# Transposing all of x by DMA rather than the first four tiles on TensorE, in a gated mix of linear attention and a token MLP

## The chip, the cores and the metric

The kernel runs on one core of a Trainium2 chip. The metric is the device time of one execution in microseconds (us), as a median. Traces have their own zero, the start of the span; a span is about 2 us shorter than the run's time. One first execution of the kernel before (963.45 us) is left out everywhere.

## The reference, cut to what matters

```
x: 2048 x 512, bf16 (16 tiles of 128 rows)
qkv = x @ wqkv;  phi(t) = where(t > 0, t + 1, exp(t)) + 1e-6
kv  = sum over s of phi(k)^T v        # per head, 32 heads of 16
a   = (phi(q) kv / phi(q) z) @ wo
b   = token MLP over the sequence of layernorm(x)   # 2048 -> 1792 -> 2048, gelu
g   = sigmoid(sum(x * gate_w));  out = g * a + (1 - g) * b
```

Only the first stage matters here: K = x Wk with its feature map phi, and G = x^T phi(K), tile by tile, with the layer-norm statistics of x beside them. K needs x transposed (`xT`), G and the statistics need plain x (`xs`).

Of the kernel before, what the change touches and what calls it, by code (L numbers as in the profile page):

```python
# [7 lines left out]
ACT = mybir.ActivationFunctionType  # L8
ALU = mybir.AluOpType
AX = mybir.AxisListType  # L10
BF16 = mybir.dt.bfloat16
# [4 lines left out]
def kernel(  # L16
# [13 lines left out]
    nc = tc.nc  # L30
    P = nc.NUM_PARTITIONS
# [8 lines left out]
    NT = S // P  # L40
    ND = D // P
# [22 lines left out]
    def keep(shape, dtype, name):  # L64
        return persist.tile(shape, dtype, name=name, tag=name)

    def bank(name, dtype=FP32):
        return ps.tile([P, SC], dtype, name=name, tag="bank")

    xs = keep([P, NT, D], BF16, "xs")  # L70
    hs = keep([P, NT, D], BF16, "hs")
    xT = keep([P, ND, S], BF16, "xT")
    wq_sb = keep([P, ND, D], BF16, "wq_sb")
    wk_sb = keep([P, ND, D], BF16, "wk_sb")
# [3 lines left out]
    pk = keep([P, NT, D], BF16, "pk")  # L78
# [9 lines left out]
    ident = keep([P, P], BF16, "ident")  # L88
# [18 lines left out]
    def mm(o, lhsT, rhs, start, stop, **kw):  # L107
        nc.tensor.matmul(o, lhsT=lhsT, rhs=rhs, start=start, stop=stop, **kw)  # L108
# [14 lines left out]
    def load_x(q, t0, n):  # L123
        q.dma_start(out=xs[:, t0 : t0 + n, :], in_=x_view[:, t0 : t0 + n, :])

    def load_wk(q, k):
        q.dma_start(out=wk_sb[:, k, :], in_=wqkv_view[:, k, D : 2 * D])

    def load_xT(t0, n):
        nc.sync.dma_start(  # L130
            out=xT[:, :, t0 * P : (t0 + n) * P], in_=X[t0 * P : (t0 + n) * P, :], transpose=True
        )

    load_x(nc.sync, 0, 1)
    load_x(nc.scalar, 1, 1)
    load_wk(nc.sync, 0)
    load_x(nc.scalar, 2, 1)
    load_x(nc.sync, 3, 1)
    for k, q in ((1, nc.scalar), (2, nc.sync), (3, nc.scalar)):
        load_wk(q, k)  # L140
    load_xT(4, 2)
    load_xT(6, 2)
    load_x(nc.sync, 4, 4)
# [5 lines left out]
    for c, (j0, nb) in enumerate(w1_chunks):  # L149
        w = wpool.tile([P, NT, FB * P], BF16, name="w1c", tag="wc")  # L150
        w1c.append(w)
        for t0 in range(0, NT, 8) if c == 0 else (0,):
            t1 = t0 + 8 if c == 0 else NT
            nc.sync.dma_start(
                out=w[:, t0:t1, : nb * P], in_=w1_view[:, t0:t1, j0 * P : (j0 + nb) * P]
# [11 lines left out]
        out=ident[:], in_=ident[:], compare_op=ALU.not_equal, fill=1.0, base=0,  # L167
# [7 lines left out]
    def load_small():  # L175
        nc.gpsimd.dma_start(out=brow[0:NF, :], in_=B_b1.rearrange("(f q) -> f q", q=P))
        nc.gpsimd.dma_start(out=brow[NF : NF + NT, :], in_=B_b2.rearrange("(f q) -> f q", q=P))
        nc.gpsimd.dma_start(
            out=gw_b[:], in_=gate_w.rearrange("(o d) -> o d", o=1).to_broadcast([P, D])
        )  # L180
# [3 lines left out]
    def warm_up(n, cols=SC):  # L184
        for _ in range(n):
            mm(wps[:, :cols], warm[:, 0:P], warm[:, :cols], True, True)

    act_warm = keep([P, 1], FP32, "act_warm")
    nc.scalar.activation(out=act_warm[:], in_=ones_f[:], func=ACT.Exp)
    warm_up(6)  # L190

    def transpose_tile(t, on_act):
        pt = bank("pt", BF16)
        for k in range(ND):
            nc.tensor.transpose(pt[:, k * P : (k + 1) * P], xs[:, t, k * P : (k + 1) * P], ident[:])  # L195
        dst = xT[:, :, t * P : (t + 1) * P]
        src = pt[:].rearrange("p (k s) -> p k s", k=ND)
        if on_act:
            nc.scalar.activation(out=dst, in_=src, func=ACT.Copy)  # L199
        else:  # L200
            nc.vector.tensor_copy(out=dst, in_=src)

    def phi(dst, acc):
        e = work.tile([P, SC], BF16, name="e", tag="e", bufs=6)
        nc.scalar.activation(out=e[:], in_=acc[:], func=ACT.Exp)  # L205
        nc.vector.tensor_scalar(  # L206
            out=e[:], in0=e[:], scalar1=1.0, scalar2=PHI_EPS, op0=ALU.min, op1=ALU.add
        )
        nc.vector.scalar_tensor_tensor(  # L209
            out=dst, in0=acc[:], scalar=0.0, in1=e[:], op0=ALU.max, op1=ALU.add  # L210
        )

    kaccs = {}

    def k_part(t, ks):
        if t not in kaccs:
            kaccs[t] = bank("kacc")
        for k in ks:
            mm(
                kaccs[t][:], xT[:, k, t * P : (t + 1) * P], wk_sb[:, k, :],  # L220
                k == 0, k == ND - 1,
            )

    def k_phi(t):
        phi(pk[:, t, :], kaccs.pop(t))

    def ln_stats(t):
        stats = work.tile([P, nc.vector.BN_STATS_DIM], FP32, name="stats", tag="stats", bufs=2)
        nc.vector.bn_stats(out=stats[:], in_=xs[:, t, :])  # L229
        nc.vector.bn_aggr(out=mv[:, t, :], in_=stats[:])  # L230

    def ln_rstd(g):
        s = slice(g * TPC, (g + 1) * TPC)
        nc.vector.tensor_scalar_add(out=veps[:, s], in0=mv[:, s, 1], scalar1=EPS)
        nc.gpsimd.tensor_tensor(out=rstd[:, s], in0=veps[:, s], in1=mhalf[:], op=ALU.pow)

    def ln_shift(g):
        s = slice(g * TPC, (g + 1) * TPC)
        nc.vector.scalar_tensor_tensor(  # L239
            out=nmr[:, s], in0=mv[:, s, 0], scalar=-1.0, in1=rstd[:, s],  # L240
            op0=ALU.mult, op1=ALU.mult,
        )

    def ln_apply(t):
        nc.scalar.activation(  # L245
            out=hs[:, t, :], in_=xs[:, t, :], func=ACT.Identity,
            scale=rstd[:, t : t + 1], bias=nmr[:, t : t + 1],
        )
# [3 lines left out]
    def g_tile(t):  # L252
        if not gacc:
            gacc.extend(bank("gacc") for _ in range(ND))
        for k in range(ND):
            mm(gacc[k][:], xs[:, t, k * P : (k + 1) * P], pk[:, t, :], t == 0, t == NT - 1)
# [15 lines left out]
    def ln_step(u):  # L272
        ln_stats(u)
        if u % TPC == TPC - 1:
            ln_rstd(u // TPC)

    HEADS = 4
    transpose_tile(0, False)
    transpose_tile(1, True)
    transpose_tile(2, False)  # L280
    ln_step(0)
    for k in range(2):
        for t in range(HEADS - 1):
            k_part(t, (k,))
    transpose_tile(HEADS - 1, True)
    ln_step(1)
    for t in range(HEADS):
        k_part(t, range(2 if t < HEADS - 1 else 0, ND))
        k_phi(t)
    LAG = 4  # L290
    LN_LAG = 3
    APPLY = 9
    for t in range(HEADS, NT):
        k_part(t, range(ND))
        k_phi(t)
        g_tile(t - LAG)
        if t > LAG:
            ln_step(t - LN_LAG)
        if t == TPC - 1 + LN_LAG:
            load_small()  # L300
        if t >= APPLY:
            ln_apply(t - APPLY)
        if t % TPC == 0 and t >= 2 * TPC:
            ln_shift(t // TPC - 2)
# [129 lines left out]
    for j in range(NB0, NF):  # L434
# [20 lines left out]
        out=gg[:], in0=gth[:], scalar1=0.5, scalar2=0.5, op0=ALU.mult, op1=ALU.add  # L455
    )
    nc.vector.tensor_scalar(
        out=c1[:], in0=gth[:], scalar1=-0.5, scalar2=0.5, op0=ALU.mult, op1=ALU.add
# [3 lines left out]
    for t in range(NT):  # L462
        c, tl = divmod(t, TPC)
        aps = bank("aps")
        for j in range(ND):
# [3 lines left out]
            out=a_sc[:], in_=aps[:], func=ACT.Identity,  # L469
            scale=gg[:, t : t + 1], bias=c2[:, t : t + 1],  # L470
        )
        for c0, W in ((0, D - P), (D - P, P)) if t == NT - 1 else ((0, D),):
            cs = slice(c0, c0 + W)
            yps = bank("yps")
            for f in range(NF):
# [6 lines left out]
                out=ot[:, :W], in0=yps[:, :W], scalar=c1[:, t : t + 1], in1=a_sc[:, cs],  # L482
# [35 lines left out]
```

## The kernel before: the parts that the change touches

The loads at the start. SP and ACT issue on two DMA rings. Tiles 0 to 3 are loaded plain, and the four chunks of Wk between them; the other tiles are transposed by the DMA.

```python
load_x(nc.sync, 0, 1)
load_x(nc.scalar, 1, 1)
load_wk(nc.sync, 0)
load_x(nc.scalar, 2, 1)
load_x(nc.sync, 3, 1)
for k, q in ((1, nc.scalar), (2, nc.sync), (3, nc.scalar)):
    load_wk(q, k)
load_xT(4, 2)          # DMA transpose of tiles 4, 5
load_xT(6, 2)
load_x(nc.sync, 4, 4)
...                    # tiles 8 to 15 in fours, then Wq, w1, Wv, Wo
```

TensorE transposes tiles 0 to 3 through PSUM, and the first chunks of Wk are used for three tiles while the others are still under way:

```python
HEADS = 4
transpose_tile(0, False); transpose_tile(1, True); transpose_tile(2, False)
ln_step(0)                                # statistics of tile 0
for k in range(2):
    for t in range(HEADS - 1):
        k_part(t, (k,))
transpose_tile(HEADS - 1, True)
ln_step(1)
for t in range(HEADS):
    k_part(t, range(2 if t < HEADS - 1 else 0, ND))
    k_phi(t)                              # exp on ACT, two steps on VectorE -> pk
LAG, LN_LAG = 4, 3
for t in range(HEADS, NT):
    k_part(t, range(ND)); k_phi(t)
    g_tile(t - LAG)                       # G needs pk of tile t - 4
    if t > LAG: ln_step(t - LN_LAG)
    ...
```

(`transpose_tile` is four PE transposes of 128x128 into a PSUM bank and one copy into `xT`, on ACT or VectorE.)

## Time and profile before

| | before |
|---|---|
| median | 165.75 us (165.62 to 165.82) |
| TensorE busy | 97% of the span |
| first stage (K and G) ends | 33.19 us |
| from there to the end of the span | 130.21 us |

The next fence is a table of stretches for the kernel before: the stretch, its length, busy us and number of instructions for TensorE, its weight loads, VectorE, ACT and GpSimd, then the granted clock, the mean share of the DMA engines and GB/s. A share over 1 is packets that overlap.

```profile
3.00:4.00 1.00, 0.72 (x4) 0.17 (x3) 0.00 (x0) 0.99 (x2) 0.17 (x2) 1.00 1.04 346
4.00:5.00 1.00, 1.00 (x12) 1.00 (x11) 0.42 (x1) 0.26 (x2) 0.00 (x0) 1.00 1.05 336
...
7.00:8.00 1.00, 1.00 (x8) 0.41 (x6) 0.33 (x2) 0.89 (x2) 0.00 (x0) 1.00 1.23 192
...
33.19:163.40 130.21, 126.77 (x641) 58.59 (x650) 61.75 (x132) 40.93 (x62) 11.13 (x18) 1.00 0.41 125
```

Plain loads alone move 346 GB/s; the microsecond in which almost only transposes run (7 to 8 us) moves 192 GB/s at a full share. The last line is all that comes after the first stage.

### The profile page before, as it was taken

To read this page: it belongs to the slowest core of one execution; us is meant where nothing else is said; L and a number is where in the kernel's file an instruction comes from. 1 tells how busy PE (TensorE), PEld (TensorE's weight loads), DVE (VectorE), ACT (ScalarE), POOL (GpSimd) and SP (SyncE) were. 2 spreads that over 40 slices of the span, in tenths; PEclk is the share of its full clock that TensorE was granted. 3 is DMA by queue.
4 is the path that set the end of the run, shared out by engine and by line. 5 is a ranking of instruction groups with operands and counts; after the bars stand their busy time and mean duration, and the time that the engine had idled before them with its cause. 6 is when DMAs were issued, how large, how long until landed. Compare 5 with 4: busy or idle time off the path is not lost.

```text
span 163.4 us, 2099 instructions
## 1 busy us (share of the span) xinstructions
PE 158.7 (97%) x787; PEld 73.3 (45%) x801; DVE 88.3 (54%) x202; ACT 58.7 (36%) x90; POOL 18.3 (11%) x37
## 2 busy tenths in 40 slices
PE   7999999999999999999999999999999999999993
PEld 2544444444444444444444444444444444444452
DVE  1599999957999999029995301156221111111112
ACT  3463386648676483111222213111112222111110
POOL 5000711200100000001055500050000000000000
PEclk9999999999999999999999999999999999999999
DMA  5999999999950007600893599932100000111001
GB/s 152 235 237 213 280 308 328 349 349 348 326 130 0 0 0 247 202 4 0 286 299 101 181 320 279 323 121 88 36 32 32 32 32 32 45 52 35 32 32 32
DMA packets 30057, 25.05 MB, mean 153 GB/s; under 512 B 7968, under 2 KB 29472, under 8 KB 30048
## 3 DMA queue, kind: packets, MB, share of 16 engines
q1 hardware_dynamic: 28032, 22.02, 45.5%
q0 software_dynamic: 1440, 2.38, 5.5%
q10 hardware_dynamic: 576, 0.52, 1.1%
q8 instruction: 6, 0.10, 0.3%
q14 instruction: 3, 0.02, 0.0%
HBM read 21.11 MB, written 2.23 MB: 143 GB/s over the span
## 4 chain that ended last, share of the span: by engine, by line
PE 95%; DMA 2%; issue 1%; ACT 0%; DVE 0%
PE uacc L108 30%; PE yps L108 29%; PE aps L108 9%; PE gacc L108 8%; PE qacc L108 8%; PE kacc L108 8%; DMA xs<-in_A_x_dram 2%; PE pt L195 1%; PE denps L108 1%; PE wps L108 1%; PE kvps L108 0%; ACT xT L199 0%; DVE ot L481 0%; PE zps L108 0%; PE pt L324 0%
## 5 line engine op out<-in xcount | busy, mean ns | idle before, releaser
L108 PE MATMUL uacc<-hs,w1c 128*128 128x512 bf16 x219 | 51.8, 379 | 0.4
L108 PE MATMUL yps<-uT,w2c 128*128 128x512 bf16 (+2 forms) x234 | 50.6, 366 | 0.2
L481 DVE SCALAR_TENSOR_TENSOR ot<-yps,c,a_sc 128x512 bf16<-128x512 f32 (+2 forms) x17 | 12.2, 720 | 46.0 <-PE yps L108 42.7
L108 PEld LDWEIGHTS <-w2c 128*128 128x128 bf16 x238 | 22.8, 98 | 25.9
L108 PEld LDWEIGHTS <-w1c 128*128 128x128 bf16 x224 | 21.7, 98 | 26.3 <-issue 0.4
L468 ACT ACTIVATE a_sc<-aps,c,gg 128x512 f32<-128x512 f32 x16 | 12.4, 778 | 46.7 <-PE aps L108 43.0
L318 ACT ACTIVATE uT<-uacc,bcol 128x512 bf16<-128x512 f32 x14 | 9.3, 687 | 28.3 <-PE uacc L108 28.3
L108 PE MATMUL aps<-W2sb,pqT 128*128 128x512 bf16 x63 | 16.4, 379 | 0.1
L108 PE MATMUL qacc<-xT,wq_sb 128*128 128x512 bf16 x63 | 16.2, 379 | 0.0
L108 PE MATMUL kacc<-wk_sb,xT 128*128 128x512 bf16 x63 | 16.0, 380 | 0.1
L108 PE MATMUL gacc<-pk,xs 128*128 128x512 bf16 x62 | 15.5, 379 | 0.1
L245 ACT ACTIVATE hs<-xs,nmr,rstd 128x512 bf16<-128x512 bf16 x16 | 12.8, 805 | 1.9 <-DVE nmr L239 1.9
L205 ACT ACTIVATE e<-qacc 128x512 bf16<-128x512 f32 x16 | 9.6, 597 | 9.2 <-PE qacc L108 8.3
L419 POOL DMA_DIRECT2D rex<-rd_dram x16 | 9.4, 602 | 23.0 <-DVE pqT L421 17.5
L205 ACT ACTIVATE e<-kacc 128x512 bf16<-128x512 f32 x16 | 9.3, 595 | 6.9 <-PE kacc L108 5.6
L209 DVE SCALAR_TENSOR_TENSOR pk<-kacc,e 128x512 bf16<-128x512 f32 x16 | 11.1, 692 | 0.6
L209 DVE SCALAR_TENSOR_TENSOR pqT<-qacc,e 128x512 bf16<-128x512 f32 x16 | 11.1, 692 | 0.6
L229 DVE BATCH_NORM_STATS2 stats<-xs 128x6 f32<-128x512 bf16 x16 | 10.9, 682 | 0.0
L206 DVE TENSOR_SCALAR e<-e 128x512 bf16<-128x512 bf16 x32 | 9.0, 282 | 3.1 <-ACT e L205 3.1
L406 DVE CUSTOM_DVE_ANT_0 junk<-xs,gw_b 128x512 bf16<-128x512 bf16 x16 | 9.9, 684 | 0.0
L270 DVE TENSOR_TENSOR zacc<-zacc,pk 128x512 f32<-128x512 f32 x14 | 9.6, 686 | 0.2
L108 PEld LDWEIGHTS <-pqT 128*128 128x128 bf16 x64 | 6.3, 98 | 7.6
(65 smaller groups left out, 69.6 us busy)
## 6 DMA issues: line engine op xcount, KB each, us to landing
w2c<-in_B_w_dram SPq DMA_DIRECT2D x8, 896.0 KB, 6.6
w1c<-in_B_w_dram SPq DMA_DIRECT2D x2, 2048.0 KB, 15.7
w1c<-in_B_w_dram SPq DMA_DIRECT2D x3, 1024.0 KB, 12.9
rex<-rd_dram POOLq DMA_DIRECT2D x16, 128.0 KB, 3.2
out_dram<-ot SPq DMA_DIRECT2D x15, 128.0 KB, 1.7
xs<-in_A_x_dram SPq DMA_DIRECT2D x3, 512.0 KB, 5.1
wq_sb<-in_A_wqkv_dram SPq DMA_DIRECT2D x1, 512.0 KB, 7.1
wv_sb<-in_A_wqkv_dram SPq DMA_DIRECT2D x1, 512.0 KB, 11.4
```

The costliest lines, as they stand in the source:

```text
L108: nc.tensor.matmul(o, lhsT=lhsT, rhs=rhs, start=start, stop=stop, **kw)
L205: nc.scalar.activation(out=e[:], in_=acc[:], func=ACT.Exp)
L206: nc.vector.tensor_scalar(out=e[:], in0=e[:], scalar1=1.0, scalar2=PHI_EPS, op0=ALU.min, op1=ALU.add)
L209: nc.vector.scalar_tensor_tensor(out=dst, in0=acc[:], scalar=0.0, in1=e[:], op0=ALU.max, op1=ALU.add)
L229: nc.vector.bn_stats(out=stats[:], in_=xs[:, t, :])
L245: nc.scalar.activation(out=hs[:, t, :], in_=xs[:, t, :], func=ACT.Identity, scale=rstd[:, t : t + 1], bias=nmr[:, t : t + 1],)
L270: nc.vector.tensor_tensor(out=zacc[:], in0=first, in1=pk[:, t, :], op=ALU.add)
L318: nc.scalar.activation(out=uT[:, j, :], in_=acc[:], func=ACT.Gelu_apprx_tanh, bias=bcol[:, j : j + 1])
L406: nc.vector.tensor_tensor_reduce(out=junk[:], in0=xs[:, t, :], in1=gw_b[:], scale=1.0, scalar=0.0, op0=ALU.mult, op1=ALU.add, accum_out=gp ...
L419: nc.gpsimd.dma_start(out=rex[:], in_=src.unsqueeze(1).to_broadcast([8, HEAD, SC]))
L468: nc.scalar.activation(out=a_sc[:], in_=aps[:], func=ACT.Identity, scale=gg[:, t : t + 1], bias=c2[:, t : t + 1],)
L481: nc.vector.scalar_tensor_tensor(out=ot[:, :W], in0=yps[:, :W], scalar=c1[:, t : t + 1], in1=a_sc[:, cs], op0=ALU.mult, op1=ALU.add,)
```

## The change

Its intent is to take the 16 transposes and their copies off the start of TensorE's work: the DMA transposes x anyhow for the later tiles, so let it do so for all. Tiles 0 and 1 come by a transpose each, ahead of everything on SP; Wk and the plain tiles 0 to 3 go to ACT's ring.

```diff
-    load_x(nc.sync, 0, 1)
-    load_x(nc.scalar, 1, 1)
-    load_wk(nc.sync, 0)
-    load_x(nc.scalar, 2, 1)
-    load_x(nc.sync, 3, 1)
-    for k, q in ((1, nc.scalar), (2, nc.sync), (3, nc.scalar)):
-        load_wk(q, k)
+    load_xT(0, 1)
+    load_wk(nc.scalar, 0)
+    load_xT(1, 1)
+    for k in range(1, ND):
+        load_wk(nc.scalar, k)
+    load_xT(2, 2)
+    load_x(nc.scalar, 0, 4)
     load_xT(4, 2)
...
-    warm_up(6)
+    warm_up(7)
...                      (transpose_tile and the interleaved head of the loop are removed)
-    for t in range(HEADS, NT):
-        k_part(t, range(ND))
-        k_phi(t)
-        g_tile(t - LAG)
-        if t > LAG:
+    for t in range(NT):
+        k_block(t)
+        if t >= LAG:
+            g_tile(t - LAG)
+        if t >= LN_LAG:
             ln_step(t - LN_LAG)
```

More of the change, by code (lines that the diff above doesn't have):

```diff
@@ L189 @@
     nc.scalar.activation(out=act_warm[:], in_=ones_f[:], func=ACT.Exp)
-    warm_up(6)
-    def transpose_tile(t, on_act):
-        pt = bank("pt", BF16)
-        for k in range(ND):
-            nc.tensor.transpose(pt[:, k * P : (k + 1) * P], xs[:, t, k * P : (k + 1) * P], ident[:])
-        dst = xT[:, :, t * P : (t + 1) * P]
-        src = pt[:].rearrange("p (k s) -> p k s", k=ND)
-        if on_act:
-            nc.scalar.activation(out=dst, in_=src, func=ACT.Copy)
-        else:
-            nc.vector.tensor_copy(out=dst, in_=src)
+    warm_up(7)
     def phi(dst, acc):
@@ L211, in phi, with k_block @@
         )
-    kaccs = {}
-    def k_part(t, ks):
-        if t not in kaccs:
-            kaccs[t] = bank("kacc")
-        for k in ks:
-            mm(
-                kaccs[t][:], xT[:, k, t * P : (t + 1) * P], wk_sb[:, k, :],
-                k == 0, k == ND - 1,
-            )
-    def k_phi(t):
-        phi(pk[:, t, :], kaccs.pop(t))
+    def k_block(t):
+        kacc = bank("kacc")
+        for k in range(ND):
+            mm(kacc[:], xT[:, k, t * P : (t + 1) * P], wk_sb[:, k, :], k == 0, k == ND - 1)
+        phi(pk[:, t, :], kacc)
     def ln_stats(t):
@@ L275, in ln_step @@
             ln_rstd(u // TPC)
-    HEADS = 4
-    transpose_tile(0, False)
-    transpose_tile(1, True)
-    transpose_tile(2, False)
-    ln_step(0)
-    for k in range(2):
-        for t in range(HEADS - 1):
-            k_part(t, (k,))
-    transpose_tile(HEADS - 1, True)
-    ln_step(1)
-    for t in range(HEADS):
-        k_part(t, range(2 if t < HEADS - 1 else 0, ND))
-        k_phi(t)
     LAG = 4
@@ L292 @@
     APPLY = 9
-    for t in range(HEADS, NT):
-        k_part(t, range(ND))
-        k_phi(t)
-        g_tile(t - LAG)
-        if t > LAG:
+    for t in range(NT):
[3 more added lines that the diff above has]
+        if t >= LN_LAG:
             ln_step(t - LN_LAG)
```

## The prediction

> **What bounds the kernel now.** I began with the page's busy shares and chain of waits. They settle where a gain can lie at all: TensorE is busy for 97% of the span, and the chain that ended last is 95% TensorE work.
>
> ```profile
> PE 158.7 (97%) x787; PEld 73.3 (45%) x801; DVE 88.3 (54%) x202; ACT 58.7 (36%) x90; POOL 18.3 (11%) x37
> PE 95%; DMA 2%; issue 1%; ACT 0%; DVE 0%
> ```
>
> What is not TensorE work on that chain is the first load. So I read the same chain in order of time (start, length, what) for the first 11 us, which is all that the change touches.
>
> ```profile
> 0.81 2.98 DMA xs<-in_A_x_dram
> 3.79 0.05 issue
> 3.84 1.05 PE pt L195 x8
> 4.89 0.02 issue
> 4.91 0.61 ACT xT L199
> 5.51 0.05 issue
> 5.56 1.29 PE kacc L108 x5
> 6.85 0.22 PE pt L195 x4
> 7.08 3.02 PE kacc L108 x14
> ```
>
> See here that nothing can start before 3.84 us, when the first tile of x has landed, and that transposing and copying out cost the chain 1.05 + 0.61 + 0.22 = 1.9 us up to 7.08. From there on it is only the K and G matmuls, four in 0.86 us (0.216 us each), until 33.19 us. The stage from the first landing to its end takes 33.19 - 3.84 = 29.35 us; its 128 K and G matmuls need 128 x 0.216 = 27.6 us. So the whole overhead of the beginning, as the kernel stands, is 1.7 us, 1% of 165.8 us.
>
> The third view is VectorE's timeline in this stage, because the page's slices show it at 9 tenths there (start, length, operation; the last lines are the end of the stage).
>
> ```profile
> 8.23 0.29 DVE L206 TENSOR_SCALAR e<-e 128x512 bf16<-128x512 bf16 x1 [0.86 <-ACT e L205]
> 8.56 0.69 DVE L209 SCALAR_TENSOR_TENSOR pk<-kacc,e 128x512 bf16<-128x512 f32 x1
> 9.17 0.28 DVE L206 TENSOR_SCALAR e<-e 128x512 bf16<-128x512 bf16 x1
> ...
> 20.07 0.29 DVE L206 TENSOR_SCALAR e<-e 128x512 bf16<-128x512 bf16 x1
> 20.39 0.69 DVE L209 SCALAR_TENSOR_TENSOR pk<-kacc,e 128x512 bf16<-128x512 f32 x1
> 21.00 0.69 DVE L229 BATCH_NORM_STATS2 stats<-xs 128x6 f32<-128x512 bf16 x1
> 21.71 0.18 DVE L230 BATCH_NORM_AGGREGATE mv<-stats 128x2 f32<-128x6 f32 x1
> 21.81 0.26 DVE L206 TENSOR_SCALAR e<-e 128x512 bf16<-128x512 bf16 x1
> ...
> 31.22 0.69 DVE L209 SCALAR_TENSOR_TENSOR pk<-kacc,e 128x512 bf16<-128x512 f32 x1
> ```
>
> A feature-map pair alone repeats every 0.93 us (8.23 to 9.17); with one layer-norm statistic it repeats every 1.74 us (20.07 to 21.81). TensorE's period is 8 x 0.216 = 1.73 us for a K and a G tile. The two engines are level, and VectorE idles nowhere from 8.23 us on. The last pk ends at 31.91 us; the G matmuls that read it start at 33.19 - 0.86 = 32.33 us. VectorE's slack at the end of the stage is thus 0.42 us. I think this is the number that decides the case.
>
> **What the Trainium skill says.** "DMA: Bandwidth & Descriptors", section "Issuing engines are not separate DMA queues", says that transfers started from different engines run on the same 16 DMA engines and interleave, and only issue time is saved. The trace agrees: from 3 to 5 us, with both rings in use, the DMA share is full at 346 and 336 GB/s. Moving the Wk chunks to ACT's ring therefore makes no bandwidth.
>
> The same page, section "Latency and other measured facts", gives DMA transposes an effective 261 GB/s. In the trace the two transposes of 256 rows (256 KB each) were issued at 3.62 and 4.97 us and landed 4.1 and 3.7 us later, at 7.7 and 8.7 us: 256 KB in 1.0 us, about 260 GB/s. It agrees, and is less than the plain loads' 346.
>
> "TensorE: Matmul & The Clock Gate", Part 1, says that matmuls run at half rate until the array has been busy for a window of about 3.4 us, and that the window runs freely. The trace has the warm-up matmuls 0.43 us apart, the first K matmul at 5.09 us at 420 ns and those after 5.5 us at 379 ns, so full rate came about 4.5 us after the first warm-up matmul. The profile's PEclk row doesn't show this. Part 4 of that page says that PE transposes do not count as busy in the same way; no run so far shows it either way.
>
> **The change part by part.**
>
> Removed from TensorE: 16 transposes. Twelve took 3.84 to 5.09 us, 1.25 us, and four took 0.22 us: 1.47 us, plus the waits for their copies. Removed beside it: two copies on ACT (2 x 0.60 us) and two on VectorE (2 x 0.42 us). VectorE's were in idle time.
>
> Added: three transposes by DMA (128, 128, 256 rows) on SP, in place of four plain loads; the plain tiles 0 to 3 are loaded too, in one piece of 512 KB, for G and the layer norm. So 0.5 MB more is moved in all, early, where the DMA engines are full. One more warm-up matmul (0.43 us) ends at about 0.84 + 7 x 0.43 = 3.9 us, before data comes: free.
>
> When does TensorE start? An issue of 256 rows took SP 1.3 us and landed 2.4 to 2.8 us after its end. For 128 rows I take half the issue, 0.65 us, and the same tail: 0.81 + 0.65 + 2.4 to 2.8 = 3.9 to 4.3 us. The Wk chunks leave ACT at about 0.80, 1.25, 1.70 and 2.15 us; before, chunks took 3.1 to 4.3 us to land, in order of issue. With that I get about 3.9, 4.6, 5.3 and 6.0 us. Here the order of work matters: before, three tiles used chunks 0 and 1 while 2 and 3 were under way; now tile 0 goes through all four chunks first. So K of tile 0 is done when chunk 3 has landed and one matmul has run: about 6.2 us. The 31 K and G groups after it need 124 x 0.216 = 26.8 us, so TensorE alone would end the stage at 33.0 us, 0.2 us earlier than now. The 1.5 us of transposes mostly turn into a wait for Wk.
>
> When does VectorE start and end? ACT's queue now issues the 512 KB load only when chunk 0 has landed (its semaphore is reused; the order of instructions shows it). That is about 4.0 + 0.6 us; then the table load, 1.28 us, and the small activation, 0.2 us: ACT is free at about 6.1 us and doesn't hold up the first exponential. That runs at 6.6 to 7.2 us (0.4 us for the last matmul's own latency, 0.60 us for itself), so VectorE begins at about 7.2 us, a microsecond earlier than 8.23. But the statistics of tiles 0 and 1, which fell in idle time before, now come into the saturated stretch: 2 x (1.74 - 0.93) = 1.6 us. Before, the stretch took 31.91 - 8.23 = 23.7 us; it becomes 25.3 us, and the last pk ends at 32.5 us. The last G tile ends 0.86 us and some 0.1 us of signal later: 33.5 us, 0.3 us **later** than now. That is above TensorE's 33.0 us and hence sets the end.
>
> Everything after this stage is unchanged TensorE work and moves with it. The sum is 165.8 + 0.3 = 166.1 us. I add 0.2 us for the risk below that is one-sided and say 166.3 us.
>
> **The rivals.**
>
> *The clock stays at half rate longer.* The warm-up now ends at 3.9 us and TensorE is then starved until about 6 us. If the window that gave full rate at about 5.3 us is not busy enough, full rate comes one window later, at about 8.7 us. Between 6.2 and 8.7 us TensorE would do 6 matmuls rather than 12, which costs 1.2 us: 167 to 167.5 us. For it: a starved array; against it: the matmuls that do run in the gap. I give it one in three.
>
> *The plain tiles 0 to 3 become the wait.* The first G group and the statistics need them at about 6.2 + 4 x 0.86 = 9.6 us. Issued at about 4.2 us, with the 4.8 to 5.1 us that such loads took, they land at 9.0 to 9.3 us. Transposes share the engines, so 1 to 2 us of stall are possible: 167 to 168 us.
>
> *A real gain.* If Wk lands faster, as ACT's ring is now Wk's alone, and K of tile 0 ends at 5.3 us, TensorE alone would end at 32.1 us, 1.1 us earlier. But VectorE would have to begin by 8.23 + 0.42 - 1.6 = 7.0 us just to break even, and ACT isn't free before about 6.1 us, so 6.7 us is the earliest: at most 0.3 us better, 165.5 us.
>
> *First transposes slow.* If a DMA transpose at the very beginning needs 5 us or more, everything slips by the excess. Nothing in the trace shows it; over 2% would take 3.3 us.
>
> **Range and chances.** The gain is capped at about 0.3 to 0.5 us by VectorE, the losses reach 2 us: 165.3 to 168.0 us. Over 2% faster (below 162.5 us) exceeds the whole overhead of 1.7 us: 0.01. Over 2% slower (above 169.1 us) needs two of the rivals together: 0.05. Within 2%: 0.94.
>
> **What would show it.** The first K matmul at about 4 us and tile 0's fourth at about 6 us, waiting for Wk; the first feature map on VectorE at about 7.2 us and then no idle time to the end; the last G tile waiting for pk; the stage's end at about 33.5 us. Matmul starts 0.43 us apart after 6 us would mean the clock rival; G's first weight load waiting on x's DMA, the second. I am wrong if the stage ends more than 2 us from 33.5 us, or if later stages change their length.

## The result, and the profile after

The changed kernel takes 168.19 us (167.36 to 168.40, four runs) against 165.75 us: 2.4 us slower, just outside the stated range. The ratio is 1.014, with a 95% interval of 1.010 to 1.018; ratios here are the mean time of one kernel's fast runs over that of the other's of the same rounds, so not quite the ratio of the medians quoted.

The page of the changed kernel, busy shares and chain by engine:

```profile
PE 159.5 (96%) x772; PEld 72.2 (43%) x786; DVE 87.4 (53%) x200; ACT 57.7 (35%) x88; POOL 18.3 (11%) x37
PE 92%; DMA 4%; SPq 2%; issue 1%; DVE 0%
```

TensorE has fewer instructions and a smaller part of the chain; DMA has 4% rather than 2%, and a new entry is SPq, time in which SP does nothing but issue. The chain in order of time says what they are (start, length, what):

```profile
0.81 1.31 SPq L130
2.11 0.06 issue
2.17 1.25 SPq L130
...
3.47 6.33 DMA xT<-in_A_x_dram
...
9.86 2.76 PE kacc L108 x12
...
31.61 4.45 PE gacc L108 x20
```

The chain before left the DMA at 3.79 us. Now SP issues two transposes for 1.3 us each, and the third, of tiles 2 and 3, is issued at 3.47 us and lands at 9.80 us. From 9.86 us on it is TensorE all the way. The first stage ends at 31.61 + 4.45 = 36.06 us, 2.87 us later than before. The waits of the changed kernel between 4 and 12 us (who for whom, total us, times, longest) name the same DMA:

```profile
PEld L108 <- DMA xT<-in_A_x_dram: 4.6, 3, 2.0
...
PE kacc L108 <- DMA xT<-in_A_x_dram: 2.0, 2, 1.1
```

The stretches of the changed kernel, with the columns of above:

```profile
6.00:7.00 1.00, 0.93 (x4) 0.21 (x2) 0.00 (x0) 0.00 (x0) 0.00 (x0) 1.00 1.05 307
...
8.00:9.00 1.00, 0.80 (x2) 0.00 (x0) 0.74 (x2) 0.16 (x1) 0.00 (x0) 1.00 1.27 90
9.00:10.00 1.00, 0.14 (x1) 0.11 (x2) 0.50 (x2) 0.43 (x1) 0.00 (x0) 1.00 1.26 278
...
36.06:166.30 130.24, 126.53 (x640) 58.52 (x649) 61.48 (x132) 40.72 (x61) 11.16 (x18) 1.00 0.39 121
```

The part after the first stage is 130.24 us long, before 130.21: all of the loss is made in the first stage. Why is the third transpose late? The DMA view of the changed kernel from 6.2 to 7.0 us has the packets, MB and share of each ring; q10 is ACT's, q1 is SP's:

```profile
q10 hardware_dynamic: 260, 0.27, 103.5%
q1 hardware_dynamic: 3, 0.00, 0.4%
```

At that time ACT's ring carries the plain x tiles 0 to 3 (Wk's last chunk landed at 6.5 us), and SP's ring, where the transpose that TensorE waits for was issued at 3.47 to 4.77 us, moves next to nothing. That suggests a theory: **the plain load on the other ring holds the transpose up.** Rivals: the transposes are slow by themselves; the clock stays at half rate (K of tiles 0 and 1 does run at 0.43 us a matmul); VectorE, as the prediction has it, sets the end.

### The profile page after: what moved, and what is told of

Read it like the earlier page. It is cut to its first block, busy times and chain, and to the rows that moved or that the text cites. A ratio compares the mean times of both kernels' runs of the same rounds, so it can differ in the third digit from the quotient of the medians.

```text
span 166.3 us, 2065 instructions
## 1 busy us (share of the span) xinstructions
PE 159.5 (96%) x772; PEld 72.2 (43%) x786; DVE 87.4 (53%) x200; ACT 57.7 (35%) x88; POOL 18.3 (11%) x37
## 4 chain that ended last, share of the span: by engine, by line
PE 92%; DMA 4%; SPq 2%; issue 1%; DVE 0%
PE uacc L108 29%; PE yps L108 29%; PE aps L108 8%; PE gacc L108 8%; PE qacc L108 8%; PE kacc L108 7%; DMA xT<-in_A_x_dram 4%; SPq L130 2%; PE denps L108 1%; PE wps L108 1%; PE kvps L108 0%; DVE ot L449 0%; PE zps L108 0%; PE pt L292 0%
## 5 line engine op out<-in xcount | busy, mean ns | idle before, releaser
L108 PE MATMUL kacc<-wk_sb,xT 128*128 128x512 bf16 x63 | 17.8, 410 | 2.2 <-DMA xT<-in_A_x_dram 2.0
L194 ACT ACTIVATE e<-kacc 128x512 bf16<-128x512 f32 x16 | 9.5, 592 | 11.1 <-PE kacc L108 11.1
L108 PEld LDWEIGHTS <-xT 128*128 128x128 bf16 x64 | 6.4, 102 | 12.2 <-DMA xT<-in_A_x_dram 4.6
L198 DVE SCALAR_TENSOR_TENSOR pqT<-qacc,e 128x512 bf16<-128x512 f32 x16 | 11.1, 692 | 0.6
L198 DVE SCALAR_TENSOR_TENSOR pk<-kacc,e 128x512 bf16<-128x512 f32 x16 | 11.1, 692 | 0.6
```

The lines of the kernel that those rows point to most:

```text
L108: nc.tensor.matmul(o, lhsT=lhsT, rhs=rhs, start=start, stop=stop, **kw)
L194: nc.scalar.activation(out=e[:], in_=acc[:], func=ACT.Exp)
L198: nc.vector.scalar_tensor_tensor(out=dst, in0=acc[:], scalar=0.0, in1=e[:], op0=ALU.max, op1=ALU.add)
```

## The experiments

Twelve kernels were run; all gave correct results. "Stage end" is the end of the first stage in the profiled run; the rest of that run's time is 131.9 to 132.5 us in every one of them, so that in the profiled runs the stage end alone decides. Landing times, too, are those of the profiled run. In f4_half and e4_both that run is the fastest of its kernel, about 1.2 us below the median, so that its times need not be those of the others. Each ratio is to the kernel before in the same rounds.

| run | edit | Wk all landed | tiles 2-3 landed | stage end | median us | ratio |
|---|---|---|---|---|---|---|
| before | | 6.5 | (PE) | 33.19 | 165.75 | |
| after | | 6.5 | 9.80 | 36.06 | 168.19 | 1.0140 |
| e1_x_behind | plain x behind transposes on SP | 6.5 | 7.4 | 34.87 | 166.92 | 1.0084 |
| f4_half | half of plain x behind | 6.3 | 8.15 | 34.40 | 167.97 | 1.0163 |
| f1_after_warm | after, 14 warm-ups | 6.5 | 9.80 | 36.06 | 167.95 | 1.0166 |
| e2_pair | tiles 0-1 in one transpose | 9.36 | 11.1 | 38.64 | 170.69 | 1.0314 |
| e4_both | e1 and e2 | 7.6 | 7.8 | 36.36 | 169.90 | 1.0249 |
| e5_wk_first | one ring, Wk first | 4.7 | 7.6 | 36.11 | 168.50 | 1.0150 |
| f3_wk_first_warm | e5, 14 warm-ups | 5.0 | 8.0 | 34.89 | 167.63 | 1.0126 |
| e3_stats_late | before, two statistics later | | (PE) | 34.19 | 166.58 | 1.0072 |
| e6_warm | e1, 14 warm-ups | 6.6 | 7.6 | 34.51 | 166.42 | 1.0048 |
| e7_warm_lag | e6, one statistic less in the stage | 6.3 | 7.2 | 34.05 | 166.21 | 1.0033 |
| e8_head3 | before, tile 3 by DMA | 7.0 | | 33.82 | 165.72 | 1.0011 |
| f2_head3_late | the same, issued later | 7.2 | | 34.15 | 165.75 | 1.0016 |

(Landing times are issue time plus time to landing, to 0.1 us.)

**e1_x_behind**

```diff
-    load_x(nc.scalar, 0, 4)
     load_xT(4, 2)
+    load_x(nc.sync, 0, 4)
```

> The changed kernel with the plain load of x tiles 0 to 3 (512 KB) taken off ACT's ring and put on SP's, behind the transposes of tiles 2 to 5. Theory 1 (the plain load, issued at 3.3 us on the other ring, holds up the transpose of tiles 2 and 3 that TensorE waits for): that transpose lands at 7 to 7.5 us rather than 9.8, the first stage ends about 2 us earlier (near 34 us, then set by VectorE), and the time is 166.0 to 166.6 us. Theory 2 (the transposes are slow by themselves, one after the other, whatever else runs): it still lands at 9.3 us or later and the time stays within 0.5 us of 168.2 us. A third possibility: x itself comes too late for the first G tile and the statistics; then the idle time moves from the weight load of xT to that of xs.

The transposes are the same and are issued at the same times, but the one of tiles 2 and 3 lands 3.9 us after its issue rather than 6.3. The view of `xT` in e1_x_behind from 3.50 to 3.60 us, when only that transpose is being issued, has it:

```profile
DMA to landing us min/median/max: 3.9/3.9/3.9
```

The two landings repeat: 9.8 us in the traces of both kernels with plain x on ACT's ring (the changed kernel and f1_after_warm), 7.2 to 7.6 us in the three with it behind (e1_x_behind, e6_warm, e7_warm_lag). The chain of e1_x_behind in order of time:

```profile
2.22 4.25 DMA wk_sb<-in_A_wqkv_dram
...
6.51 4.86 PE kacc L108 x17
...
33.85 1.02 PE gacc L108 x4
```

TensorE now waits for Wk's fourth chunk and never again for a transpose on the chain. The stage ends 1.2 us earlier and the median falls by 1.3 us (1.1 us when each is taken over the kernel before of its own rounds). Theory 1 holds, with one thing not separated: the edit puts the plain load on SP's ring and also issues it later, at 6.16 us rather than 3.34. The time is 0.3 us above what was expected, because 17 K matmuls take 4.86 us where full rate would take 3.7: half rate until about 8.7 us, which the longer wait had hidden.

**f4_half**, a half dose

```diff
-    load_x(nc.scalar, 0, 4)
+    load_x(nc.scalar, 0, 2)
     load_xT(4, 2)
+    load_x(nc.sync, 2, 2)
```

> A half dose of e1_x_behind: in the changed kernel only x tiles 0 and 1 (256 KB) stay on ACT's ring, and tiles 2 and 3 go behind the transposes on SP's. If the plain load's bytes on the other ring are what holds up the transpose of tiles 2 and 3: it lands about half way between 9.8 us (512 KB on ACT) and 7.35 us (none), at 8.3 to 8.9 us, and the time is between 166.9 and 168.2 us. If the mere presence of a plain load on the other ring does it, whatever its size: it still lands near 9.8 us. If only something at the end of the load matters: near 7.4 us.

The chain of f4_half has the landing at 3.46 + 4.69 = 8.15 us:

```profile
3.46 4.69 DMA xT<-in_A_x_dram
...
8.20 2.76 PE kacc L108 x12
```

With 0, 256 and 512 KB of plain x on the other ring it is 7.4, 8.15 and 9.80 us: it grows with the bytes, though not in a straight line, and 0.15 us below what was expected. The time is no such clean witness. The profiled run took 166.80 us at a granted clock of 1.00; the four others took 167.47 to 168.36 us, three of them at a granted clock of 0.99. What TensorE did in those is in no trace. A mean of 0.99 over 166 us is about 3.3 us at half rate, and e4_both, whose trace has the same mean, ran at half rate for 3.41 us while K was under way; so the clock is the likely cause, but that is an estimate.

**f1_after_warm**: `warm_up(7)` becomes `warm_up(14)` in the changed kernel.

> The changed kernel itself with 14 rather than 7 warm-up matmuls, nothing else. It tests the clock rival of the prediction as the cause of the loss. In the changed kernel the K matmuls of tiles 0 and 1 run at half rate, but TensorE then idles until 9.86 us for the transposed tiles 2 and 3. If that landing sets the time: the two tiles run at 0.216 us apart, the wait gets longer by as much, K of tile 2 still starts at 9.6 to 10 us, and the time stays within 0.4 us of 168.2 us. If the half rate was the cause: 1 us faster or more.

K of tiles 0 and 1 now runs at full rate (8 matmuls in 1.89 us) and the chain is the same to a hundredth:

```profile
3.47 6.33 DMA xT<-in_A_x_dram
...
9.85 2.76 PE kacc L108 x12
```

The stage ends at 36.06 us again. The median, 167.95 us, is as expected too, though its four runs spread from 167.38 to 169.66 us. The clock is not the cause in the changed kernel.

**e2_pair**

```diff
-    load_xT(0, 1)
+    load_xT(0, 2)
     load_wk(nc.scalar, 0)
-    load_xT(1, 1)
```

> The changed kernel with tiles 0 and 1 transposed by one DMA of 256 rows rather than two of 128; all else as it is. Theory 1 (a transpose takes SP about 1.3 us to issue whatever its size, so that the second small one costs 1.3 us of the queue): the next transposes are issued 1.3 us earlier, at 2.1 us, and the one of tiles 2 and 3 lands at least 1.3 us earlier than 9.8 us, at about 8 us; the time falls by 1 to 2 us, to 166.2 to 167.2 us. Theory 2 (only the plain load's bytes ahead of it matter): it lands at 9.3 us or later, and the time stays at 168.2 +- 0.5 us. On both the first K matmul is 0.3 to 0.8 us later than 4.98 us.

A miss for both theories: slower by 2.5 us than the changed kernel. The first half of theory 1 is right: 256 rows take SP 1.32 us to issue, 128 rows took 1.31, and everything behind is issued 1.3 us earlier. But then four transposes of 256 rows are under way beside Wk and plain x, and what suffers first is Wk: its fourth chunk, issued at 2.2 us, lands at 9.36 us. The DMA view of e2_pair from 5.5 to 7.5 us:

```profile
DMA packets 523, 0.25 MB, mean 123 GB/s; under 512 B 375, under 2 KB 523, under 8 KB 523
```

Both rings together move 123 GB/s. So in this trace Wk is held up as well as the transposes.

**e4_both**, both edits.

> Both edits on the changed kernel: one transpose for tiles 0 and 1, and the plain load behind the transposes of tiles 2 to 5 on SP. If the plain load and the extra issue both cost time on their own: K runs without a gap from about 6 us, VectorE sets the end of the stage at about 33 to 33.5 us, and the time is 165.5 to 166.2 us, level with the kernel before. If only one of them matters, this is within 0.4 us of the better of the two single edits.

A miss. Without the plain load, Wk still lands at 7.6 us, 1.1 us later than in e1_x_behind; that the larger transpose beside it is the reason is likely, but not shown. And TensorE, idle from 4.0 to 5.5 us, ran three matmuls at full rate, waited until 7.65 us for Wk and then ran at half rate until about 10.8 us; here the clock column shows it (K's stretches of e4_both: TensorE's busy us, clock, DMA share, GB/s):

```profile
8.00:9.00 1.00, 1.00 (x4) 0.50 1.10 349
...
11.00:12.00 1.00, 1.00 (x6) 1.00 1.12 330
```

**e5_wk_first**, on e1_x_behind

```diff
-    load_xT(0, 1)
-    load_wk(nc.scalar, 0)
-    load_xT(1, 1)
-    for k in range(1, ND):
-        load_wk(nc.scalar, k)
+    for k in range(ND):
+        load_wk(nc.sync, k)
+    load_xT(0, 2)
```

> The version with the plain load behind (e1_x_behind), with everything early on SP's ring in one order: the four Wk chunks first, then one transpose each for tiles 0-1, 2-3, 4-5, then plain x. No plain load shares the engines with a transpose from another ring. Theory 1 (plain copies and transposes served in turns from two rings slow each other: 80 to 200 GB/s in the mixed stretches of the earlier runs, against 280 for transposes alone and 346 for plain copies alone): Wk has landed by about 5.2 us, the transposes of tiles 0-1 and 2-3 by about 6.5 and 7.5 us although they are issued 1.9 us later than in e1_x_behind, where the same bytes took until 7.35 us; K runs without a gap from about 6.5 us; 166.2 to 167.2 us. Theory 2 (turns cost nothing; only bytes and issues count): the issues start 1.9 us later and so tiles 2-3 land at about 9.2 us; 168 us or more.

The landings are those that theory 1 gave: Wk at 4.7, tiles 0 and 1 at 6.2, tiles 2 and 3 at 7.6 us. But they hardly speak against theory 2, whose 9.2 us was worked out wrongly. The first transpose is issued 1.9 us later than in e1_x_behind, but the one of tiles 2 and 3 only 0.6 us later (4.05 against 3.48 us), since one issue is saved; with the 3.9 us to landing of e1_x_behind it would land at about 7.9 us. What the run does show is the order: the same 1 MB is complete at 7.6 us on one ring and at 7.4 to 7.8 us on two (e1, e4), and Wk is there 1.7 to 2.9 us earlier. The time is a miss: 168.5 us in three runs and 166.78 us in one. K's stretches of e5_wk_first show why:

```profile
7.00:8.00 1.00, 1.00 (x4) 1.00 1.10 225
```

Four matmuls in a microsecond with nothing else to do are half rate, and it lasted until about 10.4 us, after 2.3 us without work (4.0 to 6.28 us). The clock column says 1.00 all the while, but it did not measure that: the trace has no clock record before 10.16 us, and the column counts time without a record as full.

**f3_wk_first_warm**: e5_wk_first with `warm_up(14)`.

> e5_wk_first with 14 warm-up matmuls. In e5_wk_first everything had landed as expected (tile 0 at 6.3, tiles 2-3 at 7.66 us) but K ran at half rate until about 10.4 us, after 2.3 us of idle TensorE, and four of five runs took 168.5 us, one 166.8 us. If the half rate is all that e5_wk_first lost: K at 0.216 us apart from 6.3 us, no gaps, VectorE sets the end of the stage at about 34 us, 166.2 to 166.6 us, and no run near 168.5. If serving the transposes after Wk costs by itself: over 167.5 us.

K runs at full rate from 6.43 us, and the stage ends 1.2 us earlier than in e5_wk_first. The median, 167.63 us, is still 1 us above what was expected, and above the 167.5 us that was to mean that serving the transposes after Wk costs by itself. In the trace (of a run of 167.24 us) plain x lands at 11.36 us and the first G matmul waits 0.48 us for it; the rest of the excess is not explained.

**e3_stats_late**, on the kernel before: `ln_step(0)` is moved behind the fourth `k_phi`, and `ln_step(1)` into the loop, where `t > LAG` becomes `t >= LAG`.

> The kernel before, with one edit: the layer-norm statistics of tiles 0 and 1 are taken where the changed kernel takes them, in the saturated stretch of VectorE. It measures the VectorE term of the prediction by itself. As the prediction has it: 1.6 us more in the stretch less 0.42 us of slack, so the stage ends about 1.2 us later and the time is 166.8 to 167.2 us, with the last G tile waiting for pk. If VectorE has more slack than I took it to have (for example because it began later than it could): less than 0.3 us, 165.6 to 166.1 us.

The stage ends at 34.19 us, 1.0 us later than in the kernel before, and the median rises by 1.0 us. The chain of e3_stats_late at the end of the stage:

```profile
32.63 0.70 DVE pk L209
...
33.38 0.81 PE gacc L108 x3
...
34.24 0.81 PE uacc L108 x3
```

The last G tile waits for VectorE's last pk. So the VectorE term is real: two statistics in the saturated stretch cost 1.0 us beyond the slack of 0.42 us.

**e6_warm** (e1_x_behind with `warm_up(14)`) and **e7_warm_lag** (e6_warm with `LN_LAG = 4`)

> e1_x_behind with 14 rather than 7 warm-up matmuls, so that TensorE stays busy up to about 6 us, when the fourth Wk chunk lands. In e1_x_behind the K matmuls between 6.5 and 8.5 us run 0.43 us apart, half rate. If the idle time from 4.0 to 4.8 us kept the clock low: K runs at 0.216 us apart from about 6.5 us, TensorE's part ends 0.9 us earlier; but VectorE, which began at 7.76 us there and ended pk at 33.8 us, then decides, and the time falls by 0 to 0.7 us from 166.9. If the clock has another cause: still 0.43 us apart at 7 us, and no change.

> e6_warm with the layer-norm statistics one tile later behind K (4 rather than 3), so that one statistic fewer (0.8 us of VectorE) falls into the first stage. If VectorE sets the end of the stage: 0.6 to 0.8 us faster than e6_warm, until TensorE binds again at about 33.4 us, so 165.5 to 166.0 us. If TensorE or a DMA sets it: within 0.2 us of e6_warm.

e6_warm is 0.5 us faster than e1_x_behind: K runs at full rate from 6.45 us, and its chain is now VectorE's until the end of the stage:

```profile
32.74 0.70 DVE pk L198
33.44 0.04 issue
33.48 1.02 PE gacc L108 x4
```

e7_warm_lag is another 0.2 us faster by the medians (0.46 us by the stage end, of 0.6 to 0.8 expected); then TensorE binds again, with a wait of 0.24 us for plain x. It remains 0.67 us slower than the kernel before.

**e8_head3** and **f2_head3_late**, the kernel before with the DMA transposing tile 3 alone:

```diff
-    load_x(nc.sync, 3, 1)         # e8_head3 only; f2_head3_late keeps it
-    load_xT(4, 2)
+    load_xT(3, 3)
-    load_x(nc.sync, 4, 4)         # e8_head3 only
+    load_x(nc.sync, 3, 5)         # e8_head3 only
-    transpose_tile(HEADS - 1, True)
```

> The kernel before with a small dose of the change: tile 3 alone goes from TensorE's transposes to the DMA, in one transpose of 384 rows with tiles 4 and 5, behind all Wk chunks; its plain load is merged into the later one. 128 KB less stand ahead of Wk's last chunk, 4 PE transposes (0.22 us) and one copy on ACT fall away, and tile 3 is first needed at about 8.2 us. If the transposes cost only because they were put ahead of and beside what TensorE waits for: they land by 7.5 us, nothing waits, 165.2 to 165.6 us against 165.5 before. If any early transpose costs time: slower than before by 0.5 us or more.

> The kernel before with all its plain loads as they are, and tile 3 transposed by the DMA together with tiles 4 and 5 (384 rows at 3.6 us, after all Wk chunks are under way) in place of TensorE. Four PE transposes and a copy on ACT less, 128 KB of DMA more. In e8_head3 the same transpose was issued at 2.2 us, beside the Wk chunks, and these landed up to 1 us later. If it is the early mixing that costs: Wk lands by 6.5 us as before, tile 3 by about 8.1 us, and the time is 165.2 to 165.6 us, 0 to 0.3 us better than before. If tile 3 comes later than it is needed (8.0 us), TensorE idles until it lands and the time is 165.7 to 166.5 us.

Neither gains. In e8_head3 the transpose is issued at 2.2 us, and TensorE waits 1.1 us for a Wk chunk that lands at 6.64 us. In f2_head3_late Wk costs only short waits, but the transpose, issued at 3.76 us, lands at 8.89 us, and TensorE waits 0.5 us for it. The chain of f2_head3_late:

```profile
3.76 5.13 DMA xT<-in_A_x_dram
...
8.94 1.90 PE kacc L108 x8
```

Both are within 0.2% of the kernel before, with intervals of 0.9992 to 1.0030 and 1.0001 to 1.0031. No version tried beats the kernel before.

## Why the prediction was wrong

It was right on what bounds the kernel and on the rest of the kernel being carried along unchanged (130.21 and 130.24 us). Its direction was right by luck: VectorE was to set the end of the stage, and a DMA did. It was wrong on that path, and so in size: 0.3 us later was forecast for the stage, 2.87 us was measured, and the stage ended 2.56 us from the forecast 33.5 us, over the 2 us that the prediction had named as the sign of being wrong.

- **First transposes.** "For 128 rows I take half the issue, 0.65 us": it took 1.31 us, as much as 256 rows, and tile 0 landed at 4.9 us, not 3.9 to 4.3. Each of the two thus delays the issue of every later transpose by 0.65 us. The rival of a first transpose that takes 5 us or more did not occur: tile 0 landed 4.1 us after its issue.
- **Wk.** 6.0 us was forecast, 6.5 us measured. The order of work was read right: K of tile 0 waits for the fourth chunk.
- **The step that failed.** "The 31 K and G groups after it need 124 x 0.216 = 26.8 us, so TensorE alone would end the stage at 33.0 us." That takes it for granted that the transposed tiles 1 to 3 are there in time; no landing was worked out for them. Tile 1 landed at 6.7 us and tiles 2 and 3 at 9.80 us. In place of that term stands 9.86 + 120 x 0.216 = 35.8 us; the 0.3 us to the measured 36.06 us are the last matmul's own latency and some 0.1 us of waiting for pk (20 G matmuls took 4.45 us, where 20 x 0.216 is 4.32).
- **The rival that came closest** named the right load and even its landing (9.0 to 9.3 us forecast, 9.2 measured), and its 167 to 168 us came close to the result, but it had the wrong victim, so that this is luck: G did not wait for plain x; the load delayed the transposes that K needed (e1_x_behind, f4_half). The prediction also had it issued at about 4.2 us; chunk 0 landed at 3.3 us, and the load went out at 3.34 us and took 5.8 us, not 4.8 to 5.1: two errors that cancelled.
- **VectorE.** The forecast of 1.2 us for the two statistics was measured by itself as 1.0 us (e3_stats_late). In the changed kernel it was hidden behind the DMA wait but for about 0.1 us; with the wait gone it sets the end (e6_warm), as forecast. VectorE began at 7.76 us, not 7.2.
- **The clock.** Given one in three, it did occur, but in the shadow of the DMA wait, and cost nothing in the changed kernel (f1_after_warm). It cost 0.5 us in e1_x_behind.

By the medians, the 2.44 us come apart as follows: 1.1 us go with plain x on the other ring (e1_x_behind is 1.38 us over the kernel before of its rounds), 0.5 us with half rate once that is gone (e6_warm, 0.88 us over), 0.2 us with one of the two statistics (e7_warm_lag, 0.67 us over). What is left, 0.7 us, no run takes apart; the trace of e7_warm_lag has K start at 5.84 us, against 5.09 us in the kernel before, and the 0.24 us of waiting for plain x.

**What stays open.** That taking the plain load away from the transposes brings tiles 2 and 3 in 2.4 us earlier is shown by moving and halving it. Whether the other ring or only the earlier issue does the harm is not: no run keeps the load on ACT's ring and issues it later. How the engines share their turns is not shown either: from 6.2 to 7.0 us the transposes moved 3 packets, and from 8 to 9 us, with ACT's load nearly done, transposes moved only 90 GB/s where they move 278 a microsecond later. No run explains that microsecond, and such a slow spell needs no load on the other ring. In f3_wk_first_warm from 7 to 8 us only transposes moved, all from SP's ring:

```profile
DMA packets 524, 0.13 MB, mean 134 GB/s; under 512 B 524, under 2 KB 524, under 8 KB 524
```

So a part of the 2.4 us may be the transposes' own. Why f4_half's median is above e1_x_behind's by 1 us although its profiled run is not is not settled either.

## What to carry to other kernels

For every operand of the first matmuls, work out its landing, not only that of the first one: an engine that is freed of work gains nothing if its next operand comes later. A load that nobody waits for is not free when it shares the DMA engines with one that somebody waits for: here it cost the transpose 2.4 us. Put it behind; on the same ring is the one way that was tried here, and it has a price of its own, as G then waited 0.24 us (e7_warm_lag) and 0.48 us (f3_wk_first_warm) for it. And before a wait is taken away, look at what lies in its shadow: here a half-rate clock and a saturated VectorE took over part of the gain.

## What the Trainium skill lacked or had wrong

- "DMA: Bandwidth & Descriptors", section "Issuing engines are not separate DMA queues", calls issue time "usually small relative to the DMA itself". A DMA transpose took SP 1.31 us to issue for 128 rows and 1.32 us for 256, against 0.40 us for a plain load of 128 rows; three in a row held SP from 0.81 to 4.77 us. The section gives no figure for transposes.
- The same page, section "Queues, rings and completion order", has each engine take turns between rings, packet by packet. From 6.2 to 7.0 us one ring moved 260 packets and the other 3. That doesn't look like even turns, if the transposes were ready by then, which no trace shows. No page says what a transpose beside plain loads from the other ring costs: 123 GB/s for both together in e2_pair.
- "Advanced Engine Details and Errata", section "X-Bar Transpose (TRN2)", says that transpose DMAs are as fast as regular ones. Alone they moved 278 GB/s in the changed kernel (9 to 10 us), 192 in the kernel before (7 to 8 us) and 134 in f3_wk_first_warm (7 to 8 us), plain loads 346 GB/s in the kernel before. The 261 GB/s that the prediction took from the DMA page stands there for a non-contiguous middle dimension, beside 350 to 400 for the contiguous case; no run shows which of the two this is.
- "TensorE: Matmul & The Clock Gate", Part 1, warns that trace events of the clock are not to be fully trusted; it does not say that a trace may have no event for the time before the first change of rate. Here the column had 1.00 in e5_wk_first and 0.50 in e4_both, for the same 0.43 us between matmuls: the records of e5_wk_first begin at 10.16 us, those of e4_both at 3.78 us. Where there were records they agreed with the spacing (full rate from 10.16 and 10.34 us in e5_wk_first, from 8.63 and 8.83 us in e1_x_behind). For the time before the first record, go by the spacing.
